# Attention products with v issued for two blocks in turn, and other buffer counts

## The chip, the cores and the metric

The kernel runs on one core of one Trainium2 chip. The metric is the time of one execution in microseconds of device time. Before the change the median of three runs is 836.64 us (835.75 to 838.92). One execution was also profiled, and all rows below come from it.

## The reference

Three layers follow each other on 4 batches of 576 positions:

```python
scores = scale * np.matmul(q, k.transpose(0, 1, 3, 2))      # 8 heads of 64, S = 576
mask = (rel >= 0) & (rel < 64)                              # each position sees itself and the 63 before it
attn = softmax(where(mask, scores, -1e9))
x = np.matmul(attn, v)                                      # -> (4, 576, 512)

u = x + real(fft(fft(x, axis=1), axis=2))                   # mixing by a DFT
u = u + relu(layernorm(u) @ w_ch1) @ w_ch2                  # 512 -> 2048 -> 512

h = gelu(u @ w_in)                                          # 512 -> 1024, halves a, c
out = u + (a * (w_sg @ (layernorm(c) * g_ln) + b_sg)) @ w_out
```

## The kernel before

The kernel has three stages in time: attention with the DFT and the first layer norms woven in (to about 165 us), the MLP (`mlp`), and the gated layer (`gate_u`, `v_tiles`, `spatial`, `project`). Weights arrive as float64 words and are split into a high and a low float32r part by `decode`, so that most products are three matmuls (`mm3`, L113).

The change is in `attention` (L249). Because of the window, the 576 positions of a batch are cut into 9 blocks of 64, and a block sees the 128 keys that begin 64 before it. There are 36 blocks, n = 0 to 35, and j = n mod 9 is the block's place in its batch. Each block takes these steps:

- `scores` (L256): four matmuls, one for each pair of heads, write the PSUM tile `sc` [128, 4, 128] (64 queries of two heads on the partitions). VectorE adds the mask, writes `s` (SBUF, `SB` = 4 buffers) and takes the row maxima `mx` (L264). GpSimd and ScalarE make the exponentials in place in `s` (L268 to L274).
- `transposes` (L277): four TensorE transposes of `s` into the PSUM tile `pt` (one buffer), which ScalarE copies into `pts` (two buffers, L283).
- `pv` (L286): eight matmuls, one for each head, of 64 columns of `pts` with 65 columns of v (the 65th is one, and gives the sum of the row). They write 64 partitions of the PSUM tile `pv` [128, 2, 512]: partitions 0 to 63 for an even j, 64 to 127 for an odd j. In the trace each of these float32 matmuls is two weight loads (`LDWEIGHTS`) and two `MATMUL`s, 16 of each for a block. The tile has one buffer; it is allocated at an even j and shared with the next block.
- `norm` (L298), after an odd j and after the last block of a batch (j = 8, alone in its tile): VectorE adds, inverts and multiplies (L309 to L313), which gives `x` and frees `pv`.
- `xt` (L317): four TensorE transposes of `x` into the PSUM tile `xt`, copied by ScalarE into `uT`.

The loop over n (L337) writes these steps down in the order `scores(n)`, `transposes(n-1)`, `pv(n-2)`, `norm(n-2)`, `xt(n-3)` (`LAG` = 1, 2, 3). After some of them it yields a cost in ns, and `drive` (L735) then writes down steps of two other lanes for as much time: `decode` of the first MLP weights, and the DFT and layer norm of batches 0 and 1. That written order is not the final one. The program is built with `schedule_with_timeline_sim=True`: a planner goes through the instructions with its own estimate of the timeline and sets each engine's final order, the earlier written first among those that its estimate has ready. On the chip each engine then follows its own list in order and waits on semaphores.

Of the kernel before, what the change touches and what calls it, by code (L numbers as in the profile page):

```python
# [9 lines left out]
F32 = mybir.dt.float32  # L10
# [9 lines left out]
NB = S // 64  # L20
# [14 lines left out]
LAG, XPT = (1, 2, 3), 0  # L35
PACE = 1.0
XP, FP = (3, 1), ()
UB, SB, QB, VB = 3, 4, 3, 3
WARM, W0, W1 = 16, 9000, 2500
TAB_AT = (2, 4, 7, 9)  # L40
DSP, D45 = 2000, 3000
EPS = 1e-6
# [2 lines left out]


def split(a):
    """float64 -> two float32 arrays: one with 11 mantissa bits, and the rest."""
    u = a.astype(np.float32).view(np.uint32).astype(np.uint64)
    u = (u + 0x7FF + ((u >> 12) & 1)) & 0xFFFFF000  # L50
    hi = u.astype(np.uint32).view(np.float32)
    return hi, (a - hi.astype(np.float64)).astype(np.float32)
# [49 lines left out]
class Kernel:  # L102
# [8 lines left out]
        return p, es  # L111

    def mm3(self, out, terms, first=True, last=True):  # L113
        """out += sum over terms of (lh + ll) @ (rh + rl) without ll @ rl."""
        n = len(terms)
        for i, (lh, ll, rh, rl) in enumerate(terms):
            mm = self.nc.tensor.matmul
            mm(out, lhsT=lh, rhs=rh, start=first and i == 0, stop=False)  # L118
            mm(out, lhsT=lh, rhs=rl, start=False, stop=False)  # L119
            mm(out, lhsT=ll, rhs=rh, start=False, stop=last and i == n - 1)  # L120

    # ---------------------------------------------------------------- setup
    def setup(self):
        nc = self.nc
        left, right = "left", "right"
# [12 lines left out]
        self.bp, self.ndec, self.nct = None, 0, 0  # L138
        self.x2 = self.tc.dram_tile([128, 4, TOK], F32, name="x2")

    # ------------------------------------------- weights: float64 to float32r
    def decode(self, src, hi, lo, n=512, eng=None):
        """src: float64 words [128, n] in DRAM. hi + lo = src to float32's 24 bits.
        The exponent is shifted by a product, which also flushes what float32 cannot hold;
        then the bits move into float32's places."""
        nc, p = self.nc, self.pers
        for o in range(0, n, 256):
            self.ndec += 1
            q = self.bp if self.bp is not None and self.ndec % 2 else p
            s = q.tile([128, 256, 2], I32, tag="dec_s", bufs=2, name="dec_s")  # L150
            nc.sync.dma_start(s[:].rearrange("p a b -> p (a b)"), src[:, o:o + 256].bitcast(I32))
            g = p.tile([128, 256], F32, tag="dec_g", bufs=2, name="dec_g")
            w = p.tile([128, CA], I32, tag="dec_w", bufs=2, name="dec_w")[:, 0:256]
            nc.scalar.activation(out=g, in_=s[:, :, 1].bitcast(F32), func=AF.Copy, scale=2.0 ** -112)  # L154
            nc.vector.tensor_scalar(out=w, in0=s[:, :, 0], scalar1=29, scalar2=None, op0=ALU.logical_shift_right)  # L155
            nc.vector.scalar_tensor_tensor(out=w, in0=g[:].bitcast(I32), scalar=3, in1=w, op0=ALU.logical_shift_left, op1=ALU.bitwise_or)  # L156
            nc.vector.scalar_tensor_tensor(out=w, in0=s[:, :, 1], scalar=-2147483648, in1=w, op0=ALU.bitwise_and, op1=ALU.bitwise_or)
            f = w.bitcast(F32)
            nc.scalar.activation(out=hi[:, o:o + 256], in_=f, func=AF.Copy)  # L159
            (eng or nc.gpsimd).tensor_tensor(out=lo[:, o:o + 256], in0=f, in1=hi[:, o:o + 256], op=ALU.subtract)  # L160
            yield 0
# [23 lines left out]
    def gtile(self):  # L185
        return self.gps.tile([128, 512], F32, tag="g", name="g")

    # ------------------------------------------------------------ attention
    def open_attn(self):
        nc = self.nc  # L190
        self.ap_, self.attn_es = self.pool("attn", side="right")
# [17 lines left out]
        self.kt[b, g] = t  # L209

    def load_q(self, b, j, w):
        """w blocks of q from j on."""
        t, o = self.qring[(b * 5 + j // 2) % QB], j % 2
        for h in range(2):
            dst = t[64 * h:64 * h + 64, o:o + w, :, h].rearrange("d n a q -> d (n a) q")
            self.nc.sync.dma_start(dst, self.aps["q"][b, h, :, j:j + w].rearrange("d n a q -> d (n a) q"))
        for i in range(w):
            self.qt[b, j + i] = t[:, o + i]

    def load_v(self, b, j):  # L220
        """The rows of v that blocks j and j + 1 see."""
        w = min(2, NB - j)
        t = self.ap_.tile([128, 2, 520], F32, tag="v", bufs=VB, name="v")
        v = self.aps["v"][b]
        for i in range(w):
            self.vt[b, j + i] = t[:, i]
        if w == 1:
            self.nc.sync.dma_start(t[:, 0], v[64 * j:64 * j + 128, :])
        else:
            src = v[64 * j:64 * j + 128, :]  # L230
            ap = [list(x) for x in src.ap]
            src = bass.AP(tensor=src.tensor, offset=src.offset, ap=[ap[0], [64 * 520, 2], ap[1]])
            self.nc.sync.dma_start(t, src)
# [15 lines left out]
    def attention(self):  # L249
        nc, p, ps = self.nc, self.ap_, self.aps_  # L250
        st = {}
        N = B * NB
# [24 lines left out]
        def transposes(n):  # L277
            pr = st.pop(n)
            pt = ps.tile([128, 4, 128], F32, tag="pt", bufs=1 + XPT, name="pt")
            for hp in range(4):  # L280
                nc.tensor.transpose(pt[:, hp], pr[:, hp], self.ident)
            pts = p.tile([128, 4, 128], F32, tag="pts", bufs=2, name="pts")
            nc.scalar.activation(out=pts, in_=pt, func=AF.Copy)  # L283
            st[n] = pts

        def pv(n):  # L286
            b, j = divmod(n, NB)
            pts, v = st.pop(n), self.vt.pop((b, j))
            if j % 2 == 0:
                st["pv"] = ps.tile([128, 2, 512], F32, tag="pv", name="pv")  # L290
            o = st["pv"]
            r = 64 * (j % 2)
            for i in range(8):
                nc.tensor.matmul(o[r:r + 64, i // 4, 65 * (i % 4):65 * (i % 4) + 65],  # L294
                                 lhsT=pts[:, i // 2, 64 * (i % 2):64 * (i % 2) + 64],
                                 rhs=v[:, 65 * i:65 * i + 65], start=True, stop=True)

        def norm(n):  # L298
            o = st["pv"]
# [36 lines left out]
        full = lambda n: n % NB % 2 or n % NB == NB - 1  # L336
        for n in range(N + LAG[2] + 1):  # L337
            if n in TAB_AT:
                self.load_tables(TAB_AT.index(n))
            if n < N:  # L340
                scores(n)
            self.load_attn(n + 4)
            if n < N:
                yield 870
            m = n - LAG[0]
            if 0 <= m < N:
                transposes(m)
                yield 440
            m = n - LAG[1]
            if 0 <= m < N:  # L350
                pv(m)
                yield 900
                if full(m):
                    norm(m)
            m = n - LAG[2]
            if 0 <= m < N and full(m):
                xt(m)
                yield 440

    # ------------------------------------------------------------------ DFT  # L360
    def open_dft(self):
        nc = self.nc
        self.dp, self.dft_es = self.pool("dft", side="left")
# [103 lines left out]
        V.tensor_tensor(out=x[0:1, 2, 289:576], in0=pa[0:1, 287:0:-1], in1=row[:, 289:576], op=ALU.add)  # L467
        yield 2000

    # ----------------------------------------------------------- layer norm  # L470
    def open_x(self, n, p):
        """The two parts of chunk n: of the normalised rows, then of the MLP's result."""
        self.xh[n] = p.tile([128, 4, CHUNKS[n][1]], F32R, name=f"xh{n}")
        self.xl[n] = p.tile([128, 4, CHUNKS[n][1]], F32R, name=f"xl{n}")

# [5 lines left out]
        self.ctx.enter_context(es)  # L481

    def rsqrt(self, p, out, var, m, n, tag):
        """out = 1 / sqrt(var + EPS), with a Newton step."""
        V = self.nc.vector
        t = [p.tile([128, 3], F32, tag=f"{tag}{i}", name=f"{tag}{i}", bufs=2) for i in range(4)]
        v, y, c, e = (x[:m, 0:n] for x in t)
# [39 lines left out]
            V.tensor_tensor(out=self.xl[n][:, :, o:o + r], in0=pv, in1=hi, op=ALU.subtract)  # L527
            yield 1000

    # ------------------------------------------------------------------ MLP  # L530
    def open_mlp(self):
        self.bp, self.mlp_es = self.pool("mlp", side="right")
        self.bps, es = self.pool("mlp_ps", side="right", space=PSUM)
# [49 lines left out]
            second(*pend.pop(0))  # L583
            yield 1500

    # ----------------------------------------------------------------- gMLP
    def open_gmlp(self):
        nc = self.nc
        self.cp, es = self.pool("gmlp", side="right")
# [26 lines left out]
        return self.cps.tile([128, 512], F32, tag="c", name="c")  # L616

    def sg_place(self, k, p, h):
        """Where part p of K tile k of the spatial weights lies, for half h of the positions."""
        u = 2 * k + p  # L620
        i, o = ((6, 0, 1)[u // 3], S * (u % 3) + CA * h) if u < 9 else ((0, 6)[h], 3 * S)
        t = self.sets[i][:].rearrange("p a b -> p (a b)")
        return t[:, o:o + (CA, CB)[h]]
# [24 lines left out]
                yield 5 * size  # L648

    def v_tiles(self, b):  # L650
        """The normalised half v of batch b, positions on partitions; the last 64 positions
        of two batches share a tile."""
        nc, p = self.nc, self.lp
        V, A = nc.vector, nc.scalar
        o = b % 2
# [78 lines left out]


def drive(main, *lanes):
    """Trace `main` and lanes of fillers beside it; a filler gives, at each stop, how much of
    main's time goes by before it goes on."""
    credit = [0.0] * len(lanes)
    for cost in main:  # L740
        for i, fill in enumerate(lanes):
# [212 lines left out]
```

## Time and profile before

| what | value |
|---|---|
| median of three runs | 836.64 us (835.75 to 838.92) |
| the profiled execution: span from first to last instruction (the page gives no other time of it) | 837.8 us |
| TensorE matmul / weight load busy | 806.8 us (96%) / 769.5 us (92%) |
| VectorE / ScalarE / GpSimd busy | 487.7 (58%) / 279.5 (33%) / 192.0 us (23%) |
| mean granted TensorE clock | 0.988 |
| matmuls of `pv` (L294) | 576, of 6084 |

Busy time is the union of an engine's instructions. A matmul's record runs from its start to the modelled end of its results, so consecutive matmuls overlap in the records, and the engine's pace is read from the distance of their starts. PE is TensorE, PEld its weight loads, DVE VectorE, ACT ScalarE and POOL GpSimd.

### The profile page before, as it was taken

To read this page: it belongs to the slowest core of one execution; us is meant where nothing else is said; L and a number is where in the kernel's file an instruction comes from. 1 tells how busy PE (TensorE), PEld (TensorE's weight loads), DVE (VectorE), ACT (ScalarE), POOL (GpSimd) and SP (SyncE) were. 2 spreads that over 40 slices of the span, in tenths; PEclk is the share of its full clock that TensorE was granted. 3 is DMA by queue.
4 is the path that set the end of the run, shared out by engine and by line. 5 is a ranking of instruction groups with operands and counts; after the bars stand their busy time and mean duration, and the time that the engine had idled before them with its cause. 6 is when DMAs were issued, how large, how long until landed. Compare 5 with 4: busy or idle time off the path is not lost.

```text
span 837.8 us, 15602 instructions
## 1 busy us (share of the span) xinstructions
PE 806.8 (96%) x6084; PEld 769.5 (92%) x6084; DVE 487.7 (58%) x1390; ACT 279.5 (33%) x638; POOL 192.0 (23%) x238
## 2 busy tenths in 40 slices
PE   6879799889999999999999999999999999999998
PEld 6879688789999999999999999999999988889897
DVE  3586978798559556972225933553340467465643
ACT  3556555445225223531113411333232333121210
POOL 4373636243122002320002300232340021010100
PEclk9989999999999999999999999999999999999999
DMA  8996542023003002330002400132130020303032
GB/s 230 269 290 171 157 134 65 27 66 111 1 1 103 1 1 77 127 101 1 1 2 65 137 1 1 45 108 83 57 116 1 1 58 22 93 10 105 10 105 90
DMA packets 59322, 63.71 MB, mean 76 GB/s; under 512 B 22384, under 2 KB 42736, under 8 KB 59248
## 3 DMA queue, kind: packets, MB, share of 16 engines
q1 hardware_dynamic: 58672, 59.75, 24.2%
q0 software_dynamic: 576, 2.97, 1.3%
q8 instruction: 48, 0.79, 0.4%
q14 instruction: 26, 0.21, 0.1%
HBM read 53.25 MB, written 9.44 MB: 75 GB/s over the span
## 4 chain that ended last, share of the span: by engine, by line
PE 80%; DVE 8%; DMA 5%; issue 2%; POOL 1%; SPq 1%; ACT 1%; DVEq 0%; ACTq 0%; POOLq 0%
PE acc L118 7%; PE acc L120 7%; PE acc L119 7%; PE h L118 7%; PE h L120 7%; PE h L119 7%; PE c L118 6%; PE c L119 6%; PE c L120 6%; PE g L118 3%; PE g L119 3%; PE g L120 3%; PE pv L294 3%; DMA dec_s<-in_wo 2%; PE sc L260 2%
## 5 line engine op out<-in xcount | busy, mean ns | idle before, releaser
L118 PE MATMUL h<-xh,set 128*128 128x256 f32 (+1 forms) x512 | 151.5, 297 | 3.6 <-DVE rq L491 2.4
L118 PE MATMUL acc<-rh,set 128*128 128x256 f32 (+1 forms) x512 | 152.0, 297 | 0.5 <-DVE uT L556 0.5
L120 PE MATMUL acc<-rh,set 128*128 128x256 f32 (+1 forms) x512 | 151.4, 296 | 0.0
L120 PE MATMUL h<-xh,set 128*128 128x256 f32 (+1 forms) x512 | 151.4, 296 | 0.0
L119 PE MATMUL h<-xl,set 128*128 128x256 f32 (+1 forms) x512 | 151.4, 296 | 0.0
L119 PE MATMUL acc<-rl,set 128*128 128x256 f32 (+1 forms) x512 | 151.2, 295 | 0.0
L576 DVE SCALAR_TENSOR_TENSOR rl<-h,rh 128x320 fp32r<-128x320 f32 (+1 forms) x128 | 58.0, 453 | 120.3 <-ACT rh L575 120.0
L160 POOL TENSOR_TENSOR set<-dec_w,set 128x256 fp32r<-128x256 f32 x88 | 68.0, 780 | 248.4 <-ACT set L159 246.1
L575 ACT ACTIVATE rh<-h 128x320 fp32r<-128x320 f32 (+1 forms) x128 | 52.0, 406 | 165.3 <-PE h L120 119.9
L118 PEld LDWEIGHTS h<-xh,set 128*128 128x128 f32 x512 | 96.7, 189 | 4.4 <-issue 2.6
L118 PEld LDWEIGHTS acc<-rh,set 128*128 128x128 f32 x512 | 96.7, 189 | 1.1 <-issue 1.0
L120 PEld LDWEIGHTS h<-xh,set 128*128 128x128 f32 x512 | 96.8, 189 | 0.0
L119 PEld LDWEIGHTS h<-xl,set 128*128 128x128 f32 x512 | 96.8, 189 | 0.0
L120 PEld LDWEIGHTS acc<-rh,set 128*128 128x128 f32 x512 | 96.6, 189 | 0.1
L119 PEld LDWEIGHTS acc<-rl,set 128*128 128x128 f32 x512 | 96.6, 189 | 0.0
L556 DVE TENSOR_TENSOR uT<-acc,uT 128x320 f32<-128x320 f32 (+1 forms) x160 | 62.0, 448 | 13.0 <-PE acc L120 12.9
L489 POOL TENSOR_TENSOR rq<-rq,mhalf 128x1 f32<-128x1 f32 (+2 forms) x26 | 18.3, 705 | 197.3 <-DVE rq L488 194.2
L154 ACT ACTIVATE dec_g<-dec_s 128x256 f32<-128x256 f32 x88 | 38.3, 438 | 70.0 <-DVE dec_w L156 34.1
L118 PE MATMUL c<-xh,set 128*128 128x256 f32 (+1 forms) x188 | 55.4, 295 | 0.0
L120 PE MATMUL c<-xh,set 128*128 128x256 f32 (+1 forms) x188 | 55.3, 294 | 0.0
L119 PE MATMUL c<-xl,set 128*128 128x256 f32 (+1 forms) x188 | 55.3, 294 | 0.0
L155 DVE TENSOR_SCALAR dec_w<-dec_s 128x256 int32<-128x256 int32 x88 | 35.7, 406 | 32.8 <-POOL set L160 21.0
(193 smaller groups left out, 1669.3 us busy)
## 6 DMA issues: line engine op xcount, KB each, us to landing
dec_s<-in_w SPq DMA_DIRECT2D x64, 256.0 KB, 2.7
v<-in_v SPq DMA_DIRECT2D x16, 520.0 KB, 5.1
k<-in_k SPq DMA_DIRECT2D x11, 512.0 KB, 6.3
dec_s<-in_wi SPq DMA_DIRECT2D x16, 256.0 KB, 2.7
q<-in_q SPq DMA_DIRECT2D x30, 128.0 KB, 6.2
x<-uT SPq DMA_DIRECT2D x4, 640.0 KB, 3.9
out<-uT SPq DMA_DIRECT2D x4, 640.0 KB, 4.0
dec_s<-in_wo SPq DMA_DIRECT2D x8, 256.0 KB, 2.8
```

The source lines that it names most:

```text
L118: mm(out, lhsT=lh, rhs=rh, start=first and i == 0, stop=False)
L119: mm(out, lhsT=lh, rhs=rl, start=False, stop=False)
L120: mm(out, lhsT=ll, rhs=rh, start=False, stop=last and i == n - 1)
L154: nc.scalar.activation(out=g, in_=s[:, :, 1].bitcast(F32), func=AF.Copy, scale=2.0 ** -112)
L155: nc.vector.tensor_scalar(out=w, in0=s[:, :, 0], scalar1=29, scalar2=None, op0=ALU.logical_shift_right)
L160: (eng or nc.gpsimd).tensor_tensor(out=lo[:, o:o + 256], in0=f, in1=hi[:, o:o + 256], op=ALU.subtract)
L260: nc.tensor.matmul(sc[:, hp], lhsT=q[:, hp].rearrange("p a b -> p (a b)"), rhs=k[:, hp, o:o + 128], start=True, stop=True)
L294: nc.tensor.matmul(o[r:r + 64, i // 4, 65 * (i % 4):65 * (i % 4) + 65], lhsT=pts[:, i // 2, 64 * (i % 2):64 * (i % 2) + 64], rhs=v[:, 65 * ...
L489: self.nc.gpsimd.tensor_tensor(out=y, in0=v, in1=self.mhalf[:m, 0:n], op=ALU.pow)
L556: V.tensor_tensor(out=x, in0=acc[:, c, 0:size], in1=x, op=ALU.add)
L575: A.activation(out=rh, in_=o, func=AF.Relu)
L576: V.scalar_tensor_tensor(out=rl, in0=o, scalar=0.0, in1=rh, op0=ALU.max, op1=ALU.subtract)
```

## The change

`pv(n)` is now called only after an odd j and for the last block of a batch. Called for an odd j it takes both blocks n-1 and n, and for each head issues the matmul of the even block (to partitions 0 to 63 of the tile) and then that of the odd block (to partitions 64 to 127). The tile `pv` is allocated in that call. `pts` gets three buffers instead of two, and `s` three instead of four (`SB`). The yield after `pv` is 1800 ns for a pair and 900 ns for a single block; the call that was there for an even j, with its yield, is gone. Beside that the diff only removes comments.

```diff
-UB, SB, QB, VB = 3, 4, 3, 3
+UB, SB, QB, VB = 3, 3, 3, 3
...
-            pts = p.tile([128, 4, 128], F32, tag="pts", bufs=2, name="pts")
+            pts = p.tile([128, 4, 128], F32, tag="pts", bufs=3, name="pts")
...
         def pv(n):
             b, j = divmod(n, NB)
-            pts, v = st.pop(n), self.vt.pop((b, j))
-            if j % 2 == 0:
-                st["pv"] = ps.tile([128, 2, 512], F32, tag="pv", name="pv")
-            o = st["pv"]
-            r = 64 * (j % 2)
+            both = [n - 1, n] if j % 2 else [n]
+            ops = [(64 * (m % NB % 2), st.pop(m), self.vt.pop((b, m % NB))) for m in both]
+            st["pv"] = o = ps.tile([128, 2, 512], F32, tag="pv", name="pv")
             for i in range(8):
-                nc.tensor.matmul(o[r:r + 64, i // 4, 65 * (i % 4):65 * (i % 4) + 65],
-                                 lhsT=pts[:, i // 2, 64 * (i % 2):64 * (i % 2) + 64],
-                                 rhs=v[:, 65 * i:65 * i + 65], start=True, stop=True)
+                for r, pts, v in ops:
+                    nc.tensor.matmul(o[r:r + 64, i // 4, 65 * (i % 4):65 * (i % 4) + 65],
+                                     lhsT=pts[:, i // 2, 64 * (i % 2):64 * (i % 2) + 64],
+                                     rhs=v[:, 65 * i:65 * i + 65], start=True, stop=True)
...
-            if 0 <= m < N:
+            if 0 <= m < N and full(m):
                 pv(m)
-                yield 900
-                if full(m):
-                    norm(m)
+                yield 1800 if m % NB % 2 else 900
+                norm(m)
```

## Rows read from the trace of the kernel before

**Rows 1.** Stretches: us, busy us (instructions) of each engine, granted clock, DMA share, GB/s

```profile
0.00:32.00 32.00, 23.99 (x220) 21.58 (x220) 14.46 (x90) 13.16 (x29) 11.80 (x30) 1.00 0.97 254
32.00:166.00 134.00, 118.96 (x1105) 106.25 (x1106) 104.61 (x385) 71.97 (x164) 64.27 (x80) 0.94 0.54 149
166.00:180.00 14.00, 10.59 (x72) 10.04 (x71) 13.58 (x27) 4.84 (x14) 7.53 (x5) 0.99 0.12 39
180.00:838.00 658.00, 653.28 (x4691) 631.63 (x4689) 355.08 (x891) 189.55 (x433) 108.37 (x124) 1.00 0.17 53
```

**Rows 2.** Chain of waits, 32 to 166 us: shares by engine and line

```profile
by line: PE pv L294 19.8%; PE sc L260 12.6%; DMA q<-in_q 8.0%; PE xt L323 6.1%; PE pt L281 5.6%; DVE s L264 5.5%; DVE E L397 5.0%; issue 4.5%; PE g L118 4.3%; PE g L120 3.7%; PE g L119 3.6%; DVE dec_w L156 2.8%; DVE dec_w L155 2.3%; DVE uT 
```

**Rows 3.** Stretches of 20 us inside attention, columns as in rows 1

```profile
60.00:80.00 20.00, 20.00 (x197) 18.37 (x198) 11.28 (x53) 13.64 (x34) 6.69 (x10) 1.00 0.74 190
80.00:100.00 20.00, 17.02 (x160) 15.27 (x158) 19.25 (x59) 11.44 (x27) 12.76 (x14) 1.00 0.67 198
100.00:120.00 20.00, 16.44 (x140) 14.32 (x141) 17.38 (x75) 10.38 (x23) 9.67 (x14) 0.83 0.38 113
120.00:140.00 20.00, 20.00 (x193) 18.53 (x192) 13.90 (x56) 11.39 (x28) 8.27 (x9) 1.00 0.27 82
140.00:160.00 20.00, 17.26 (x165) 14.68 (x164) 15.32 (x39) 8.04 (x15) 9.62 (x13) 0.91 0.13 40
```

**Rows 4.** Timeline of PE, 72 to 81 us: start, us, line, operation, tiles, count

```profile
72.42 1.05 PE L260 MATMUL sc<-k,q 128*128 128x128 f32 x8
73.31 0.60 PE L281 MATMUL pt<-ident,s 128*128 128x128 f32 x4
...
77.19 0.60 PE L281 MATMUL pt<-ident,s 128*128 128x128 f32 x4
77.72 1.15 PE L294 MATMUL pv<-v,pts 128*64 128x65 f32 x16
78.80 1.16 PE L260 MATMUL sc<-k,q 128*128 128x128 f32 x8
79.79 0.60 PE L281 MATMUL pt<-ident,s 128*128 128x128 f32 x4
80.23 1.06 PE L260 MATMUL sc<-k,q 128*128 128x128 f32 x8
```

**Rows 5.** All weight loads and matmuls of `pv`: min/median/max ns, first and last start

```profile
L294 PEld LDWEIGHTS pv<-v,pts x576: 132/138/232, 15.0 to 161.7; 128*64 128x64 f32 x192
L294 PE MATMUL pv<-v,pts x576: 219/222/370, 15.0 to 161.7; 128*64 128x65 f32 x192
```

**Rows 6.** Timeline of PE, 46 to 48 us: blocks 9 and 10 without work between

```profile
46.17 1.90 PE L294 MATMUL pv<-v,pts 128*64 128x65 f32 x32
48.01 0.82 PE L260 MATMUL sc<-k,q 128*128 128x128 f32 x5
```

**Rows 7.** Timeline of PE, 5 ns wide, at 47.11 and at 60.71 us: matmuls in flight

```profile
46.92 0.40 PE L294 MATMUL pv<-v,pts 128*64 128x65 f32 x7
...
60.49 0.40 PE L294 MATMUL pv<-v,pts 128*64 128x65 f32 x4
```

**Rows 8.** Matmuls of `pv` alone by stretch: us, busy (count), clock, DMA

```profile
0.00:32.00 32.00, 6.87 (x96) 1.00 0.97 254
...
62.50:80.00 17.50, 4.80 (x64) 1.00 0.69 169
...
118.00:163.00 45.00, 14.30 (x192) 0.96 0.20 61
```

**Rows 9.** Who waited for whom, 32 to 166 us: total us, times, longest

```profile
DVE rc L309 <- PE pv L294: 9.2, 7, 2.6
...
PE sc L260 <- DVE mx L264: 6.5, 4, 3.1
...
DVE s L264 <- PE pt L281: 5.5, 5, 2.3
```

**Rows 10.** Timeline of PE around 102 us; in brackets the idle time before and its releaser

```profile
97.81 1.16 PE L260 MATMUL sc<-k,q 128*128 128x128 f32 x8 [1.95 <-DVE mx L264]
102.05 2.07 PE L260 MATMUL sc<-k,q 128*128 128x128 f32 x8 [3.08 <-DVE mx L264]
104.06 2.00 PE L294 MATMUL pv<-v,pts 128*64 128x65 f32 x16
```

**Rows 11.** Stretches in which the granted clock was half, columns as in rows 1

```profile
53.40:60.10 6.70, 5.33 (x30) 4.58 (x30) 6.26 (x32) 2.11 (x6) 5.15 (x7) 0.50 1.04 291
101.20:107.90 6.70, 5.85 (x38) 5.17 (x39) 6.38 (x18) 2.15 (x4) 2.60 (x3) 0.50 0.17 39
```

**Rows 12.** Timeline of DVE at 78 us: a block's first score head

```profile
77.93 0.29 DVE L264 CUSTOM_DVE_ANT_0 s<-sc,mask 128x128 f32<-128x128 f32 x1 [2.31 <-PE pt L281]
```

## The prediction

> **What bounds the kernel now.** I read the busy times by stretch first [rows 1]. From 180 us to the end TensorE is busy for 653.28 of 658 us. That part issues the same instructions after the change, so the change can only move the moment at which it begins. From 0 to 32 us the DMA engines are 97% busy and no engine is: that stretch waits for q, k, v and tables, and shorter matmuls gain nothing there. From 166 to 180 us VectorE is busy for 13.58 of 14 us; this stretch holds no attention and moves as a whole. What is left is 32 to 166 us, where TensorE is busy 118.96 us and VectorE 104.61 us of 134.
>
> The chain of waits through it [rows 2] has `pv` as its largest piece: 19.8% of 134 us, 26.5 us. In stretches of 20 us [rows 3] two kinds alternate. At 60 to 80 and 120 to 140 us TensorE is busy all the time and VectorE only 11.28 and 13.90 us; at 80 to 100 and 100 to 120 us VectorE is busy 19.25 and 17.38 us and TensorE has gaps; 140 to 160 us lies between, nearer to the first kind.
>
> **The change part by part.**
>
> *What a run of `pv` costs now.* A matmul of `pv` is 222 ns long [rows 5], and a run of 16 is 1.15 us from first start to last end [rows 4]. So 16 starts are about (1.15 - 0.22) / 16 = 0.058 us apart, 0.93 us for the run. The run takes more than that out of its surroundings. From 77.19 to 79.79 us there are a group of `pt`, a run of `pv` and a group of `sc`, 2.60 us. Without `pv` beside them `pt` takes 80.23 - 79.79 = 0.44 us and `sc` 73.31 - 72.42 = 0.89 us [rows 4]. The run costs 2.60 - 0.44 - 0.89 = 1.27 us: 0.93 for its matmuls and 0.34 for going into 64 weight columns and out again. A pair of blocks costs 2.54 us.
>
> *What a pair costs in turn.* The matmuls of the two blocks write different halves of the partitions. At one end they overlap fully: 16 steps of 0.058 with both halves in each, one step more to fill, one entry and exit: 0.93 + 0.06 + 0.34 = 1.33 us, 1.21 less than now. At the other end they don't overlap: 32 x 0.058 + 0.34 = 2.20 us, 0.34 less. Below nothing I find no row: the weight loads and matmuls stay 16 + 16 of each. The trace has one place that decides between the ends: the runs of blocks 9 and 10, which write opposite halves, follow each other without work between [rows 6], and where they meet seven matmuls are in flight at one instant, against four inside a single run [rows 7]; four is what 222 / 58 gives. At the seam the two halves do work side by side, though block 10's matmuls were written after block 9's. The 32 took 48.01 - 46.17 = 1.84 us with the exit, less than twice the 1.08 us from a run's start to the next group (78.80 - 77.72, rows 4). I take the full overlap, 1.21 us a pair.
>
> The trace speaks here against a rule. The Trainium skill, "TensorE: Matmul & The Clock Gate", Part 3 (What overlaps and what doesn't), says that weight loads overlap with matmuls in flight only where the row group differs; here the column group alone differs, so by this rule the turns gain nothing, which is the second rival below. The seven in flight [rows 7] do not agree with it.
>
> *How much of it is on the path.* There are 16 pairs and 4 single blocks. Three pairs (96 matmuls) lie before 32 us and gain nothing [rows 8]. The stretches bound by TensorE hold 64 matmuls, two pairs, at 62.5 to 80 us, and 192, five pairs and two single blocks, at 118 to 163 us [rows 8]. 7 x 1.21 = 8.5 us. VectorE has room to follow: 11.28 + 2 x 1.21 stays far below 20 in the first, and what it waits for there is largely `pv` itself (9.2 us in 7 waits, rows 9). The other six pairs after 32 us lie where VectorE is busy or DMA is: I count them at nothing, at most at 6 x 1.21 = 7.3 us, and with them 1.7 us for two runs saved at half clock (2.00 us instead of 1.15, rows 10, two of them).
>
> *Moves.* The even block's matmuls come a step later. Nobody waits for them alone: `norm` comes after the odd block as before. The pair is queued on TensorE where the odd run was, and takes 1.33 us instead of 1.27: `xt` and the next `sc` behind it are 0.06 us later at most. The tile `pv` (one buffer) is first written a step later after the `norm` that frees it, which only helps. GpSimd's, ScalarE's, VectorE's and DMA's instructions stay as they are; the v tiles of an even block are held a step longer, hidden as the loads of v come in pairs of blocks anyway.
>
> *Buffers.* A third `pts` pays for the even block that now waits for its partner: block n+3's copy needs the pair's matmuls, as it needed block n+1's before. Value 0. The fourth `s` that is taken away is a price. VectorE now waits for `pt` to free an `s` in 5 places, 5.5 us in total [rows 9], 2.31 us in one [rows 12], with four buffers; so scores run ahead as far as the ring lets them, and with three they run one block less ahead. Free of cost if all of that is slack; at the other end each of the 30 blocks after 32 us waits 1.1 us (5.5 / 5), 33 us, of which VectorE's idle time in that stretch (134 - 104.61 = 29.4 us) can hide nearly all. I take 1.5 us on the path, nearer to the free end, because the trace shows this wait mostly where TensorE, not VectorE, sets the pace.
>
> *Sum.* 8.5 - 1.5 = 7.0 us. The span of the profiled execution, 837.8 us, is 1.2 us above the median of the runs; it becomes 830.8, and the median 836.64 becomes 829.6 us, 0.8% less.
>
> **The rivals.**
>
> *Nothing to be had: VectorE and the score ring set the pace.* For it: VectorE is busy for 78% of 32 to 166 us, and TensorE's waits there are for `mx` [rows 9]. Against it: two of the stretches show TensorE without a gap. It leaves a third of the 8.5 us, less the ring's 1.5: 1.3 us, 835.3 us.
>
> *No overlap, or the turns don't come about.* By the rule above, or if the planner, which has the even block's `pts` ready a step earlier, puts its matmuls ahead on their own where it sees TensorE idle. Against the second: a run of `pv` in the trace comes behind other TensorE work, not at once when it is ready. With only the 0.34 us of entry and exit for 7 pairs it is 2.4 us, less part of the ring's price: 835 us.
>
> *Slower: the score ring runs dry and the clock falls.* At 97.81 and 102.05 us TensorE sat idle 1.95 and 3.08 us for `mx` while VectorE worked on the DFT, and then had half the clock, 1.2 GHz, for 6.7 us [rows 10, 11], which costs up to 3.35 us: 8.4 us for one such event. With one block less ahead in the ring, and TensorE with fewer matmuls to fill its time, two more of them would come. From one on the gain of 7.0 is gone; with two it is 836.6 - 7.0 + 16.8, some 846 us; I give it 844 with part of the second hidden. Against it: with four buffers there are only two stretches of this length at half clock [rows 11], though VectorE already waits for the ring in five places.
>
> *All of it counts.* 13 pairs and the half clock: 15.7 + 1.7 = 17.4 us, 819.2 us.
>
> **How the numbers follow.** Forecast (own range 823 to 832.4): 0.52. All of it: 0.06. VectorE sets the pace: 0.13. No overlap: 0.12. Slower: 0.17. What a measurement can tell from no change is about 0.5%, 4.2 us, so below 832.4 is faster and above 840.8 slower. Faster 0.52 + 0.06 = 0.58, same 0.13 + 0.12 = 0.25, slower 0.17. The range of 8 in 10 leaves out about half of "all of it" and most of "slower": 820 to 842 us.
>
> **What would show it.** In the profile after: runs of 32 matmuls of `pv` that last about 1.2 us, with seven or eight in flight; the stretch up to the MLP's first matmul (165 us now) shorter by 7 us and the rest of equal length; `pv` in the chain at well under 26.5 us. Runs of 32 that last 2 us refute the overlap; runs of 16 of one block refute the turns; a longer total for VectorE's wait for `pt` or more time at half clock shows the ring's price. If `pv` shrinks and the MLP begins no earlier, the bound was VectorE.

## The result and the profile after

The changed kernel takes 829.74 us (median; 825.84 to 835.18) against 837.78 us before: ratio 0.9897, interval 0.9862 to 0.9931. Measured once more beside other kernels (experiment 5) it was 0.9932, 0.9907 to 0.9957. So by these two measurements it is faster by 5.7 to 8.6 us, 0.7% to 1.0%; 7.0 was forecast.

Stretches of the changed kernel's profile (columns as in [rows 1]), cut where its MLP's first matmul starts, at 156.59 us (165.43 before), and then 160 us later:

```profile
0.00:32.00 32.00, 24.98 (x225) 21.85 (x225) 14.64 (x91) 13.84 (x31) 12.14 (x31) 0.95 0.98 250
32.00:157.00 125.00, 107.98 (x1085) 94.25 (x1086) 103.48 (x379) 69.02 (x159) 67.67 (x80) 0.93 0.61 161
157.00:317.00 160.00, 157.36 (x1194) 153.26 (x1194) 112.91 (x277) 56.00 (x137) 35.10 (x41) 1.00 0.13 41
317.00:833.00 516.00, 511.66 (x3585) 491.49 (x3583) 255.20 (x645) 139.09 (x314) 80.33 (x88) 0.99 0.18 56
```

Of the 134 us in [rows 1] 125 are left up to there. TensorE is busy for 11 us less, VectorE for only 1 us less. What comes behind attention did not get shorter. This profiled execution took 835.18 us, the longest of its kernel, and one reason is visible: TensorE spent 6.8 us at half clock at 680 us, far behind the change (last section).

A pair in the changed kernel, from its timeline of PE, and the matmuls in flight in 5 ns at 46.70 us:

```profile
46.17 1.16 PE L294 MATMUL pv<-v,pts 128*64 128x65 f32 x32 [1.71 <-DMA v<-in_v]
47.26 0.66 PE L281 MATMUL pt<-ident,s 128*128 128x128 f32 x4
...
46.48 0.43 PE L294 MATMUL pv<-v,pts 128*64 128x65 f32 x8
```

32 matmuls last 1.16 us where 16 lasted 1.15 [rows 4], with eight in flight where four were [rows 7]. To the next group it is 47.26 - 46.17 = 1.09 us; a single run had 78.80 - 77.72 = 1.08. A whole pair costs what a block did. The row also shows something new: `pv` waited 1.71 us for v.

The planner did not keep every pair whole. Three of the 16 ran as one run of 32, as the one above. In seven the even block's first head came ahead on its own; in four of these the other 30 matmuls then ran in one run (1.15 us). In the remaining nine pairs, three of the seven among them, other work of TensorE came between the pieces. One of the four:

```profile
24.57 0.33 PE L294 MATMUL pv<-v,pts 128*64 128x65 f32 x2
...
25.64 1.15 PE L294 MATMUL pv<-v,pts 128*64 128x65 f32 x30
```

Waits of the changed kernel from 32 to 166 us, answering to [rows 9]:

```profile
DVE s L264 <- PE pt L281: 8.2, 6, 2.5
...
PE pt L281 <- ACT pts L283: 4.6, 3, 2.0
PE xt L323 <- DVE x L313: 4.1, 3, 3.4
DVE rc L309 <- PE pv L294: 3.9, 4, 1.7
```

VectorE's wait for `pv` fell from 9.2 to 3.9 us, and its wait for `pt` to free an `s` rose from 5.5 to 8.2.

### The profile page after: what moved, and what is told of

Same layout as the page of the kernel before. It is cut to its first block, busy times and chain, and to the rows that moved or that the text cites. A ratio compares the mean times of both kernels' runs of the same rounds, so it can differ in the third digit from the quotient of the medians.

```text
span 833.3 us, 15597 instructions
## 1 busy us (share of the span) xinstructions
PE 802.0 (96%) x6084; PEld 760.9 (91%) x6084; DVE 486.2 (58%) x1390; ACT 277.9 (33%) x638; POOL 195.2 (23%) x238
## 5 line engine op out<-in xcount | busy, mean ns | idle before, releaser
L160 POOL TENSOR_TENSOR set<-dec_w,set 128x256 fp32r<-128x256 f32 x88 | 70.7, 809 | 241.7 <-ACT set L159 239.0
L155 DVE TENSOR_SCALAR dec_w<-dec_s 128x256 int32<-128x256 int32 x88 | 37.6, 430 | 34.1 <-POOL set L160 23.1
```

## Experiments

Every ratio is to the kernel before on the same chip, with its 95% interval. The three columns behind it are from each kernel's profile: when the MLP's first matmul starts; how long it is from there to the last 3584 matmuls (the same matmuls in all kernels, but for 4 to 27 at its beginning); and how long from there to the end.

| kernel | ratio (interval) | first MLP matmul at | middle | rest |
|---|---|---|---|---|
| before | 1 | 165.4 | 159.0 | 513.4 |
| changed (first profile) | 0.9897 (0.9862 to 0.9931) | 156.6 | 160.3 | 516.4 |
| 1 blocks one after the other | 0.9969 (0.9949 to 0.9989) | 161.8 | 160.2 | 514.0 |
| 2 four `s`, `gr` with `mi` | 0.9962 (0.9943 to 0.9982) | 154.2 | 166.3 | 514.5 |
| 3 `pv` twice | 1.0039 (1.0021 to 1.0057) | 170.3 | 156.8 | 516.2 |
| 4 before, buffers only | 0.9995 (0.9971 to 1.0019) | 161.1 | 160.3 | 517.7 |
| 5 changed again | 0.9932 (0.9907 to 0.9957) | 155.6 | 160.4 | 514.5 |
| 6 `gr` with `mi`, three `s` | 0.9995 (0.9974 to 1.0015) | 156.6 | 166.5 | 513.6 |
| 7 yields as before | 0.9889 (0.9866 to 0.9912) | 153.9 | 160.4 | 514.6 |
| 8 pairs across batches | 0.9982 (0.9966 to 0.9998) | 149.8 | 172.2 | 515.0 |
| 9 `gr` in `E`, three `s` | 0.9941 (0.9919 to 0.9963) | 155.1 | 160.5 | 515.5 |
| 10 `gr` in `E`, four `s` | 0.9893 (0.9867 to 0.9918) | 152.6 | 160.6 | 514.0 |
| 11 the same, yields as before | 0.9952 (0.9926 to 0.9979) | 154.8 | 164.4 | 514.1 |
| 12 pairs across batches, four `s`, yields | 1.0017 (0.9993 to 1.0042) | 149.7 | 174.1 | 515.6 |

Two things help to read the table. In the kernel before and in 3 the middle has 15 matmuls less than in the changed kernel, because they run ahead of the MLP's first one; at 0.11 to 0.12 us from start to start that is some 1.7 us (an estimate), which moves from the middle into the column before it. And the granted clock differs from kernel to kernel: its mean over the runs is 0.987 before, 0.989 for the changed kernel, 0.992 in 1, 0.993 in 3, 0.991 in 4 and 0.992 in 7. A difference of 0.005 is worth up to 4 us of 836.

The theory: the two halves of the partitions overlap, TensorE has less to do in attention, and about half of that reaches the end. The main rivals: the later call and the buffers do it, or a lucky order of the planner.

**1. The two blocks one after the other.**

```diff
-            for i in range(8):
-                for r, pts, v in ops:
+            for r, pts, v in ops:
+                for i in range(8):
```

> The changed kernel with the two blocks of a pair issued one after the other, all 8 heads of the even block and then all 8 of the odd one; buffers, yields and the place of the call stay. Theory (the two halves of the partitions overlap and that shortens TensorE): a pair is about 2.0 us instead of 1.2 (only the seam overlaps, and one entry and exit is saved), so most of the gain goes: 2 to 3 us below the kernel before, ratio 0.995 to 0.999. Rival (the later call, the freer tile pv and the third pts make the gain, not the turns): ratio as the changed kernel's, 0.990.

Measured 0.9969, 2.6 us less than before. All matmuls of `pv` up to 166 us: before, changed, and this kernel (us, busy and count, clock, DMA):

```profile
0.00:166.00 166.00, 44.15 (x576) 0.95 0.62 169
```

```profile
0.00:166.00 166.00, 30.36 (x576) 0.94 0.65 171
```

```profile
0.00:166.00 166.00, 41.57 (x576) 0.97 0.67 170
```

Of the 13.8 us that the change takes from these matmuls' busy time, 11.2 come from the turns. By the medians the rest of the edit keeps 2.6 us (0.9 to 4.3 by the interval) of 8.6 or 5.7, so the turns make the larger part. The interval overlaps a little with that of experiment 5, but the stage tells the two kernels apart. Without turns the MLP begins at 161.1 to 165.4 us (before, 1, 4); in the ten profiles with turns, 3 aside, at 149.7 to 156.6.

What makes the 2.6 us is not shown. It need not be the freer `pv` tile, for TensorE had a higher clock here. From 32 us to the MLP's first matmul, in this kernel and then in experiment 4:

```profile
32.00:161.80 129.80, 114.52 (x1114) 101.51 (x1112) 104.62 (x386) 71.22 (x161) 66.05 (x81) 0.97 0.62 159
```

```profile
32.00:161.10 129.10, 113.30 (x1081) 101.26 (x1080) 101.25 (x376) 68.70 (x157) 66.62 (x79) 0.96 0.59 154
```

0.97 against 0.94 [rows 1] over 130 us is up to 4 us. The gain of the turns does not come from the clock: the changed kernel had 0.93 in this stretch, no more than the kernel before, and its last `pv` still ended 8.3 us earlier (153.7 against 162.0).

**2. Four buffers for `s`, first try.** The room for it came from letting a one-partition tile of the DFT share a place.

```diff
-UB, SB, QB, VB = 3, 3, 3, 3
+UB, SB, QB, VB = 3, 4, 3, 3
...
-        gr = p.tile([1, 290], F32, tag="gr", name="gr")
+        gr = p.tile([128, 290], F32, tag="mi", name="gr")[0:1]
```

> The changed kernel with the fourth buffer for s given back (three pts stay; the 1-partition tile gr of the DFT shares the place of mi to make room). Theory (the ring of three costs a little): 1 to 2 us below the changed kernel, ratio to the kernel before about 0.988. Rival (the ring is slack): as the changed kernel, 0.990. Third (the scores run too far ahead with four): slower than the changed kernel, over 0.992.

Measured 0.9962, slower than the changed kernel: a miss, and the third expectation by its number. But its attention ended earlier than the changed kernel's (154.2 against 156.6) and the middle was 6 us longer. Experiment 6 shows why.

**3. `pv` issued twice.**

```diff
-            for i in range(8):
+            for i in [*range(8)] * 2:
```

> The changed kernel with the matmuls of pv issued a second time over the same results: 20 runs get 16 more steps of 0.058 us, 18.6 us more of TensorE in all. Theory (about half of TensorE's time in this stretch is on the path): 8 to 11 us more than the changed kernel, ratio to the kernel before 1.000 to 1.004. Rival (VectorE now sets the pace and TensorE has room): at most 3 us more, ratio below 0.994.

```profile
0.00:171.00 171.00, 49.42 (x1152) 0.96 0.63 165
```

Measured 1.0039, which is 0.0107 to 0.0142 or 9 to 12 us above the changed kernel, for 49.42 - 30.36 = 19.1 us more of busy time. So half to two thirds of this added time reached the end; it can be more, as the runs had a higher clock than the changed kernel's (0.993 against 0.989, up to 3 us). VectorE alone does not set the pace.

**4. The kernel before with the buffer counts of the change.**

```diff
-UB, SB, QB, VB = 3, 4, 3, 3
+UB, SB, QB, VB = 3, 3, 3, 3
...
-            pts = p.tile([128, 4, 128], F32, tag="pts", bufs=2, name="pts")
+            pts = p.tile([128, 4, 128], F32, tag="pts", bufs=3, name="pts")
```

> The kernel before with the buffer counts alone (three s, three pts). Theory (the turns make the gain, the shorter ring of s costs 1.5 us): 0 to 2 us slower than before, ratio 1.000 to 1.003. Rival (the third pts makes the gain): ratio 0.990 to 0.994. Second rival (the ring runs dry and the clock falls): over 1.005.

Measured 0.9995: no difference. The counts alone give no time, against the rival. In its profile the MLP does begin 4.4 us earlier than before, but 1.7 us of that is the moved 15 matmuls, the clock in attention was higher (0.96 against 0.94, up to 3 us), and the rest is 4.3 us longer, with 6.8 us at half clock at 686 us.

**5. The changed kernel again,** as reference of 6 to 8.

> The changed kernel once more, on the chip of the three beside it, as their reference. Both theories: ratio to the kernel before 0.987 to 0.993.

Measured 0.9932. Its profile has no half clock between attention and the last microseconds, and a span of 830.4 us against 833.3.

**6. The shared place alone** (the second edit of 2, with three `s`).

> The changed kernel (three s) with the one edit that made room for the fourth s: the DFT's small tile gr shares the place of mi. In the run with four s attention ended 2.4 us earlier than in the changed kernel, and the 80 us behind it gave back 6. Theory (that shared place costs: the DFT of the next batch waits for it): 3 to 6 us slower than the changed kernel, ratio to before 0.994 to 0.997. Rival (the four s themselves, through the order of the work behind attention, cost it): as the changed kernel, 0.987 to 0.993.

Measured 0.9995: the whole gain is gone, through an edit that has nothing to do with attention. VectorE's timeline in this kernel around 210 us:

```profile
209.57 1.05 DVE L460 TENSOR_TENSOR uT<-uT,pl 128x289 f32<-128x289 f32 x1
...
210.60 0.44 DVE L408 TENSOR_TENSOR gr<-O 1x288 f32<-1x288 f32 x1
211.08 0.76 DVE L411 TENSOR_TENSOR O<-O 128x576 f32<-128x576 f32 x1
211.87 0.45 DVE L410 TENSOR_TENSOR grow<-gr,grow 1x289 fp32r<-1x289 f32 x1
212.33 1.68 DVE L555 TENSOR_TENSOR uT<-acc,uT 128x320 f32<-128x320 f32 x4
213.93 0.68 DVE L526 TENSOR_TENSOR xl<-g,xh 128x512 fp32r<-128x512 f32 x1
```

and the same place in the changed kernel (experiment 5):

```profile
208.46 1.05 DVE L460 TENSOR_TENSOR uT<-uT,pl 128x289 f32<-128x289 f32 x1
210.76 0.69 DVE L526 TENSOR_TENSOR xl<-g,xh 128x512 fp32r<-128x512 f32 x1 [1.25 <-ACT xh L525]
```

By the code `gr` of the next DFT now has to wait until `mi` has been read. Its chain lands ahead of the layer norm's `xl`, which comes 3.2 us later, of which 1.0 us was there at the MLP's first matmul (156.6 against 155.6). TensorE in this kernel waits for it:

```profile
214.76 0.36 PE L429 MATMUL g<-tab,grow 128*128 128x258 f32 x1 [1.10 <-DVE xl L526]
...
264.60 0.46 PE L523 MATMUL g<-ident,u 64*128 64x64 f32 x4 [0.85 <-DVE xl L526]
```

These waits and the like are half of the longer middle: TensorE has nothing at work for 5.8 of 166.5 us, against 2.7 of 160.3 in experiment 5. The other half is the clock. Within 2 us after each of the two waits shown it fell to half for 3.4 us, which is worth up to 3.4 us in all; experiment 5 has full clock in its whole middle. This kernel at the two places and in its middle, then experiment 5 in its middle:

```profile
215.20:218.60 3.40, 3.40 (x19) 3.40 (x18) 0.56 (x2) 0.39 (x1) 0.00 (x0) 0.50 0.02 6
266.40:269.80 3.40, 2.98 (x14) 3.01 (x15) 1.88 (x5) 0.60 (x1) 0.00 (x0) 0.50 0.15 54
156.60:323.10 166.50, 160.75 (x1197) 156.52 (x1196) 113.92 (x278) 57.21 (x137) 34.78 (x41) 0.98 0.12 39
```

```profile
155.60:315.90 160.30, 157.58 (x1197) 153.44 (x1195) 113.30 (x278) 56.08 (x137) 35.50 (x41) 1.00 0.13 41
```

So 2 and 6 have the same long middle, and only their difference speaks of the `s`: 0.0033, and 2.4 us in attention.

**7. The yields of the kernel before.**

```diff
-                yield 1800 if m % NB % 2 else 900
+            if 0 <= m < N:
+                yield 900
+            if 0 <= m < N and full(m):
                 norm(m)
```

> The changed kernel with the yields of the kernel before (900 ns after every block's place, the even ones too, in place of 1800 after a pair): the same instructions, the other lanes written down at slightly different places. It measures what a new order alone does. Theory (the gain is TensorE's time in attention): within 2 us of the changed kernel, ratio to before 0.988 to 0.993. Rival (the gain is a lucky order): over 0.995.

Measured 0.9889, by the medians 3.1 us faster than experiment 5 beside it (the intervals overlap). The gain stays under this other order, so it was no lucky one. Whether this order by itself is worth the 3 us is not shown: the runs' clock was higher too (0.992 against 0.989, up to 3 us).

**8. Pairs across the batches.** Blocks 2i and 2i + 1 of all 36, and v loaded to suit.

```diff
-            both = [n - 1, n] if j % 2 else [n]
-            ops = [(64 * (m % NB % 2), st.pop(m), self.vt.pop((b, m % NB))) for m in both]
+            both = [n - 1, n]
+            ops = [(64 * (m % 2), st.pop(m), self.vt.pop(divmod(m, NB))) for m in both]
...
-            t0 = S * b + 128 * i
+            t0 = 64 * (n - 1)
...
-            if j == NB - 1:
-                self.xdone = b
+            self.xdone = (n + 1) // NB - 1
...
-        full = lambda n: n % NB % 2 or n % NB == NB - 1
+        full = lambda n: n % 2
```

> The changed kernel with pairs across the batches too: blocks 2i and 2i + 1 of all 36, so 18 pairs and no single block, 18 runs of norm and xt in place of 20, and v loaded so that pairs of odd batches lie in one tile. Theory (TensorE's time in attention counts for about half to two thirds): two runs of 1.3 us, half of two groups of xt and two norms of VectorE (1.1 us each) less, 2 to 3 us faster than the changed kernel, ratio to before 0.984 to 0.988. Rival (VectorE or the order behind attention sets the end): as the changed kernel, 0.989 to 0.993.

Measured 0.9982, a miss: attention ends 6 to 7 us earlier than in the changed kernel, more than expected, and the middle takes it all back. In this kernel's middle TensorE waits for VectorE's part of the MLP and of the layer norm:

```profile
149.80:322.00 172.20, 162.32 (x1208) 157.93 (x1208) 117.91 (x286) 59.28 (x140) 36.62 (x42) 0.98 0.13 40
...
156.91 0.62 PE L118 MATMUL h<-xh,set 128*128 128x320 f32 x1 [3.18 <-DVE rl L572]
...
187.72 0.66 PE L520 MATMUL g<-ident,u 128*128 128x128 f32 x4 [1.36 <-DVE xl L523]
```

10 us of the 172.2 have no TensorE at work; in the changed kernel it was 2.6 of 160. Of these 172.2 us 6.8 were at half clock, up to 3.4 us more, where the changed kernel's middle had none.

**9 and 10. Four `s` again, with another place for `gr`:** the dead end of the DFT's tile `E`, two columns wider. 9 has this alone, 10 with four `s`.

```diff
-        E = p.tile([128, 2, S], F32, tag="E", name="E")
+        Et = p.tile([128, 2, S + 2], F32, tag="E", name="E")
+        E = Et[:, :, 0:S]
...
-        gr = p.tile([1, 290], F32, tag="gr", name="gr")
+        gr = Et[0:1, 1, 289:578]
```

> The changed kernel (three s) with the DFT's small tile gr moved into two columns more of the tile E, whose part there is dead by then: it frees the same place as sharing with mi did, without that wait. It is the reference of the next run. Theory (sharing with mi made a new wait, the place alone costs nothing): as the changed kernel, ratio to before 0.987 to 0.994. Rival (any new order behind attention costs): 0.994 to 1.000.

> The same with four s. Theory (the ring of three costs 2 to 3 us in attention, as the two runs with the shared place differ by 0.0033): 2 to 3 us faster than the run beside it, ratio to before 0.985 to 0.991. Rival (the ring is slack and the difference was order): as the run beside it.

Measured 0.9941 and 0.9893: 0.0048, 4 us, and the intervals just do not overlap. In attention it is 155.1 against 152.6. VectorE's wait for `pt`, 32 to 166 us, in 9 and then in 10:

```profile
DVE s L264 <- PE pt L281: 4.9, 5, 2.6
```

```profile
DVE s L264 <- PE pt L281: 0.9, 1, 0.9
```

So the fourth `s` is worth 2.4 to 2.5 us in attention and 3 to 4 us in all. Experiment 10 and experiment 7 have the lowest medians (828.63 and 828.92 us), but neither is clear of the changed kernel's first measurement.

**11 and 12. The edits together:** 10 with the yields of 7; and the same with the pairs of 8.

> The same with four s and 900 ns yielded after every block's place, as in the run with those yields. Theory (the effects add: 0.0033 for the ring, 0.0043 for the yields): ratio to before 0.982 to 0.987, faster than every kernel so far. Rival (each is an accident of the planner's order and they do not add): 0.987 to 0.995.

> Pairs across the batches (18 pairs, no single block), with the four s, gr in E and the 900 ns yields. In the run of these pairs alone attention ended 3.5 us earlier than in the changed kernel and the layer norms and DFTs behind it gave 7 us back. Theory (that was the order behind attention, which another writing order changes): 0.980 to 0.987. Rival (pairs across batches end batch 0 a block later, so its DFT always comes at a worse place): 0.992 to 1.000.

Measured 0.9952 and 1.0017. Both are misses: the effects do not add. In 11 attention ends 2 us later than in 10 and the middle is 4 us longer; in 12 attention ends earliest of all, at 149.7, and the middle is longest, 174.1. As in 6 and 8, TensorE waits there (it has nothing at work for 5.6 us in 11 and 11.9 in 12) and has half the clock for a time (6.8 us in 12).

## Why the prediction was right, point by point

**The overlap** is right: eight matmuls in flight, 32 in the time of 16. The rule of the Trainium skill that the prediction sets against it ("TensorE: Matmul & The Clock Gate", Part 3, What overlaps and what doesn't) does not agree with these rows. The term of 1.21 us a pair comes out at 1.26 where a pair is whole (2 x 1.27 before, 1.27 + 0.01 after, an estimate). The rival that the turns don't come about did in part: only three pairs stayed whole.

**How much is on the path** came near in its sum, in part by luck, and is wrong in its places. Compare VectorE's multiplication in the `norm` of three pairs (blocks 15 and 16, 22 and 23, 33 and 34), before and then after:

```profile
79.34 0.69 DVE L313 TENSOR_TENSOR x<-pv,rd 128x512 f32<-128x512 f32 x1
...
118.04 0.68 DVE L313 TENSOR_TENSOR x<-pv,rd 128x512 f32<-128x512 f32 x1
...
159.90 0.69 DVE L313 TENSOR_TENSOR x<-pv,rd 128x512 f32<-128x512 f32 x1
```

```profile
77.91 0.69 DVE L313 TENSOR_TENSOR x<-pv,rd 128x512 f32<-128x512 f32 x1
...
113.62 0.69 DVE L313 TENSOR_TENSOR x<-pv,rd 128x512 f32<-128x512 f32 x1
...
151.62 0.69 DVE L313 TENSOR_TENSOR x<-pv,rd 128x512 f32<-128x512 f32 x1
```

The gain is 1.4 us by 79 us, 4.4 by 118 and 8.3 by 160. I had counted two pairs at 60 to 80 us in full, 2.4 us; the whole of the first 79 us gave 1.4. I had counted the VectorE-bound stretch from 80 to 118 us at nothing; it gave 3.0. The five pairs behind were to give 6.05 and gave 3.9. A busy share in 20 us does not tell which stretch pays. Experiment 3 gives a share for the whole, half to two thirds, and no places.

The luck is in the sum. The last `pv` ends 8.3 us earlier than before, and 9.3 in experiment 5, with the ring's price already taken off. Without that price (2.4 us, next point) it would be some 11 us, an estimate, where I had 8.5. A gain that was taken too small, a price that was taken too small, and some us that the later stages gave back cancel nearly.

**The ring's price** has the right sign and is too small: 1.5 us forecast, 2.4 to 2.5 measured in attention (2 against 6, 9 against 10), and VectorE's wait rose as the row said it would. The clock does not make this difference: from 32 us to the MLP's first matmul TensorE had half the clock for 3.4 us less in 2 than in 6, and for 6.8 us more in 10 than in 9. The slower rival, which needed 8 us or more from it, is refuted: the granted clock from 32 us to the end of attention is 0.93 against 0.94 [rows 1].

**The entry and exit** (0.34 us a run) is not measured apart; experiment 1 keeps what is saved of it and the overlap at the seam, and is 2.6 us below the kernel before, with a higher clock.

**Missed: v.** I wrote that holding the v tiles longer is hidden. It cost one wait of 1.71 us, in the stretch in which DMA is busy.

**Missed: the middle.** "The rest of equal length" holds for the changed kernel: 160.3 against 159.0 us is no more than the 15 matmuls moved into the middle (some 1.7 us), and the rest is 514.5 against 513.4 in experiment 5. That the middle can be 174 us long with almost the same matmuls, by the planner's order of the last two DFTs and layer norms and the half clock behind TensorE's waits, was in no rival. Nor was a granted clock that differs between kernels by up to 4 us' worth, except as something that makes the kernel slower.

**The span.** I took it as 1.2 us above the run's time. In the later profiles an execution is 1.7 to 1.9 us longer than its span (835.18 and 833.3, for one); the difference forecast does not hang on it.

What stays open: what makes the 2.6 us of experiment 1, whether the higher clock in 1, 3, 4 and 7 comes from their order of work, and why the same edits end in one order of the middle or the other. The runs show the price of an order, not the planner's reason; and the two causes of the order in 8 and 12 (batch 0 ready a block later, or other places of the lanes) were not told apart.

## What to carry to other kernels

Two float32 products of 64 output partitions each, written in turn to the lower and the upper half, took the time of one here, wherever they ran without other work between; look for the seam where two such runs already meet to see it before building it. Where two engines share a stretch about evenly, don't assign the time removed to places; doubling the work in question measures in one run what share of it reaches the end, here about half to two thirds. Time a change in stages: an edit that shortens one stage may be paid back in the next by another order of work and the waits and half clock that come with it, up to its whole gain (experiments 6, 8 and 12). And read the granted clock beside every small difference: in experiment 1 it could be the whole of the 2.6 us.

## What the runs showed of the hardware that was not expected

The clock can halve while TensorE's records show no gap. The changed kernel's first profile at 680 us:

```profile
680.20:686.80 6.60, 6.60 (x26) 5.71 (x26) 5.51 (x15) 1.62 (x4) 0.00 (x0) 0.50 0.01 1
673.00:680.00 7.00, 7.00 (x41) 5.61 (x40) 4.16 (x9) 2.26 (x5) 0.00 (x0) 1.00 0.16 49
```

41 matmuls in the 7.0 us before it, 26 in 6.6 us at 1.2 GHz. Busy is not the same as full pace, though. From 677 us to the fall the starts are 0.3 us apart and more, where they were 0.12 us apart just before; products of 128 and of 64 rows follow each other there in turn:

```profile
676.56 0.29 PE L119 MATMUL c<-set,set 128*128 128x256 f32 x1
676.68 0.28 PE L120 MATMUL c<-set,vl 128*128 128x256 f32 x1
...
677.84 0.41 PE L706 MATMUL c<-set,vtail 64*128 64x320 f32 x1
678.18 0.41 PE L705 MATMUL c<-set,vtail 128*128 128x320 f32 x1
```

Experiment 4 has the same half clock at 686 us and experiment 9 half as much of it at 680. The other profiles don't, though experiment 5's, of the same kernel, has the same slow stretch; so whether the clock falls there belongs to the execution. It costs up to 3.3 us, as much as half of what is measured here. The changed kernel's first four runs lie 9.3 us apart, the slowest with a clock of 0.984 and the fastest with 0.991.
